# Sorted k of the late pairs copied into block order, so that the score matmuls read a block's columns side by side

## The chip, the cores and the metric

The kernel runs on one core of one Trainium2 chip. The metric is the time of one execution on the device, in microseconds (us). Most executions of this kernel agree within a few tenths of a per cent, but single ones are about 2 us longer with a mean granted TensorE clock of 0.99 in place of 1.00 (the kernel before, in one set of rounds: 226.22 us at 0.990 beside 223.60 to 224.78 at 0.997 and more; one more, 227.03 us at 0.990, was called slow and is left out of the ratios). Ratios in this document are the mean time of one kernel's fast runs over the mean of the other's fast runs of the same rounds, so they are not quite the ratios of the medians quoted beside them.

## The reference, cut to what matters

```python
# q, k, v: (4 batches, 8 heads, 768 positions, 64); sort_net: 8x8 per head; 8 blocks of 96 positions
for _ in range(5):                       # Sinkhorn normalisation of sort_net -> P
    ...
k_sorted = einsum('bhij,bhjcd->bhicd', P, k_b)   # mix the 8 blocks of k (and of v) by P
v_sorted = einsum('bhij,bhjcd->bhicd', P, v_b)
scores = scale * (q_block @ k_sorted_block^T)    # within each block only, 96 x 96
attn = softmax(scores)
x = (attn @ v_sorted_block)  -> (3072 tokens, 512)
out = square(relu(x @ w_in)) @ w_out             # 512 -> 2048 -> 512
```

The feed-forward part is most of the work. The attention of batch n+1 is woven into the feed-forward matmuls of batch n.

## The kernel before

A small planner inside the kernel decides the order of all instructions before anything runs. Each piece of work is given an engine, an estimated cost and the pieces it depends on. Pieces for TensorE also carry a due time, counted in chunks of feed-forward work. A transfer is a pseudo engine with a cost and a slack. In the traces VectorE, ScalarE and TensorE work their queues in order: what the planner puts first has to finish first, whatever really happens.

Two heads make a pair. For the ten late pairs (two of batch 1, four each of batches 2 and 3), k is sorted in natural order, transposed by a DMA from SyncE's queue, and lands in `kx` with the 8 blocks interleaved: column `8 x + i` belongs to block `i`. The score matmuls therefore read every eighth column:

```python
rkx, rkn, rqi = Ring(3), Ring(4), Ring(4)          # buffers: transposed k, natural k, paired q
...
def s_turn(b, hp):
    ...
    sp = plan.add("SP", 1.25, k_turn, [op, loaded(b)] + oldx)      # issue of the DMA transpose
    k_op = plan.add("WAY", 1.6, lambda e: None, [sp])              # its way, as planned
...
nc.tensor.matmul(out=scp[:, h, BLK * n:BLK * (n + 1)],
    lhsT=(u.ksT[64*h:64*(h+1), HS*hf + BLK*n:HS*hf + BLK*n + 128] if not u.tiled else
          kx_r[u.kx][64*h:64*(h+1), NQ*hf + n::NB]),               # step of 8 columns
    rhs=..., start=True, stop=True)
...
# sorted v of a batch: written to DRAM and read back in another layout, from SyncE's queue
slow = 6.0 if b == 1 else 2.0
there = plan.add("WAY", slow, ..., [wr]);  back = plan.add("WAY", slow, ..., [rd])
```

Early pairs have k in `kvT`, where a block's columns lie side by side. That gives a control inside the same trace.

The softmax here doesn't subtract the row's maximum and nothing guards it: scores larger than these inputs give would overflow.

Of the kernel before, what the change touches and what calls it, by code (L numbers as in the profile page):

```python
# [9 lines left out]
BF16 = mybir.dt.bfloat16  # L10
# [8 lines left out]


DUES = {
    (0, "K"): (-15.0, -1.0, 10, 10),
    (0, "S"): (-1.0, 11.0, 11.0, 15.0),
    (0, "T"): (-1.5, 10.0, 13.5, 19.5),
    (0, "A"): (14.0, 14.5, 18.0, 21.5),
    (0, "X"): (16.0, 23.0, 24.5, 25.0),
    (0, "W"): (1.5,),
    (1, "V"): (4.0, 20.5),
    (1, "Q"): (31.0,),
    (1, "N"): (None, 33.0),  # L30
    (1, "Z"): (None, None, 43.0, 44.0),
    (1, "S"): (33.5, 41.0, 43.0, 48.0),
    (1, "A"): (39.5, 41.5, 45.5, 52.0),
    (1, "X"): (48.0, 49.5, 49.5, 55.0),
    (2, "L"): (52.0,),
    (2, "N"): (64.0, 69.5),
    (2, "V"): (74.5, 91.5),
    (2, "Z"): (84.0, 86.0, 95.5, 96.5),
    (2, "S"): (88.5, 93.0, 97.5, 100.5),
    (2, "A"): (95.0, 99.5, 102.0, 104.0),  # L40
    (2, "X"): (96.5, 105.5, 107.5, 109.5),
    (3, "L"): (110.5,),
    (3, "N"): (120.0, 126.0),
    (3, "V"): (123.0, 141.5),
    (3, "Z"): (130.5, 138.0, 153.0, 155.5),
    (3, "S"): (143.5, 153.0, 157.5, 159.5),
    (3, "A"): (149.5, 155.0, 160.5, 162.5),
    (3, "X"): (158.5, 160.0, 161.5, 166.5),
}



FIRST = ("K0 V0 K1 v1 S0 t0 S1 k2 t1 A0 V2 S2 K3 t2 A1 V3 X0 A2 S3 t3 x1 A3 X2 x3")


class Op:
# [35 lines left out]
class Plan:  # L92
# [1 line left out]



    TAIL = {"PE": 0.0, "ACT": 0.09, "DVE": 0.06, "POOL": 0.0, "DMA": 0.0, "SP": 0.0, "WAY": 0.6}
    HOP = 0.06
    SWITCH = 0.1
    SLACK = {"DMA": 2.5, "WAY": 1.0}  # L100

    def __init__(self):
        self.att, self.ffn, self.rest = [], [], []
# [62 lines left out]
def kernel(  # L166
# [10 lines left out]
    nc = tc.nc  # L177

    B, H, S, D = q.shape
    NB = sort_net.shape[-1]  # L180
    BLK = S // NB
    NH = B * H
    NA = S // 128
    C0 = 128 // NB
    HP = H // 2
    NQ = NB // 2
    HS = S // 2
# [7 lines left out]
    const = ctx.enter_context(tc.tile_pool(name="const", bufs=1))  # L195
# [15 lines left out]
    plan = Plan()  # L211
    rvn, rvb = Ring(2), Ring(3)
    r1, r2, rf, rh1, rh2, rob = Ring(1), Ring(2), Ring(3), Ring(3), Ring(2), Ring(3)
    rqT, rao, rks, ret = Ring(6), Ring(3), Ring(3), Ring(4)
    rkx, rkn, rqi = Ring(3), Ring(4), Ring(4)
    AD = ("ACT", "DVE")

    def cost_f(n):
# [8 lines left out]
    def copy(eng, out, in_):  # L227
        if eng == "ACT":
            nc.scalar.copy(out=out, in_=in_)  # L229
        else:  # L230
            nc.vector.tensor_copy(out=out, in_=in_)  # L231
# [40 lines left out]
    v_way = nc.dram_tensor("v_way", (B, 2, NA, 128, HP * 66), BF16, kind="Internal").ap()  # L272

    kn_r = [const.tile([128, NA, 2, D], BF16, name=f"kn{n}") for n in range(4)]
    qi_r = [const.tile([128, NA, 2, D], BF16, name=f"qi{n}") for n in range(4)]
    kx_r = []
    for n in range(3):
        kx = const.tile([128, 128 * NB], BF16, name=f"kx{n}")
        nc.vector.memset(kx[:, 128 * NA:], 0.0)
        kx_r.append(kx)  # L280
    for n in range(4):
        et = const.tile([96, 2, HS + 32], BF16, name=f"et{n}")
        nc.vector.memset(et[:, :, HS:HS + 32], 0.0)
# [331 lines left out]
    def s_sc(u, due=0):  # L615

        u.exps = {}
        u.et = {}
        for hf in u.halves:
            st = {}  # L620

            slot, old = r2.take()

            def mm(e, hf=hf, st=st, slot=slot):
                qT = tiles["qT", u.b, u.hp]
                if not u.tiled:
                    qT = qT.rearrange("p a x -> p (a x)").rearrange("p (i q) -> p i q", q=BLK)
                st["p"] = scp = p2[slot]
                for n in range(NQ):
                    for h in range(2):  # L630
                        nc.tensor.matmul(  # L631
                            out=scp[:, h, BLK * n:BLK * (n + 1)],
                            lhsT=(u.ksT[64 * h:64 * (h + 1), HS * hf + BLK * n:HS * hf + BLK * n + 128]
                                  if not u.tiled else
                                  kx_r[u.kx][64 * h:64 * (h + 1), NQ * hf + n::NB]),
                            rhs=(qT[64 * h:64 * (h + 1), NQ * hf + n, :] if not u.tiled else
                                 qT[64 * h:64 * (h + 1), :, C0 * (NQ * hf + n):
                                    C0 * (NQ * hf + n + 1)]),
                            start=True, stop=True)

            s2 = slot
            u.et[hf], olde = ret.take()
            pe = plan.add("PE", 0.17 if not u.tiled else 0.26, mm, [u.k_op, u.q_op] + old, due,
                          mode="row")
            r2.use(s2, pe)
            rqT.use(qTs[u.b, u.hp], pe)
            if not u.tiled:
                rks.use(u.n, pe)
            else:
                rkx.use(u.kx, pe)  # L650
            u.exps[hf] = []
            if u.b == 0:
                def ex(e, st=st, et=et_r[u.et[hf]]):
                    nc.scalar.activation(out=et[:, :, 0:HS], in_=st["p"][0:96, :, 0:HS],  # L654
                                         func=AF.Exp, scale=scale)

                op = plan.add("ACT", cost_f(2 * HS)[0], ex, [pe] + olde)
                r2.use(s2, op)
                u.exps[hf].append(op)
                continue  # L660
            for h in range(2):
                def ex(e, h=h, st=st, et=et_r[u.et[hf]]):
                    nc.scalar.activation(  # L663
                        out=et[:, h, 0:HS].rearrange("p (n c a) -> p n c a", c=C0, a=NA),
                        in_=st["p"][0:96, h, 0:HS].rearrange("p (n a c) -> p n c a", c=C0, a=NA),
                        func=AF.Exp, scale=scale)
                op = plan.add("ACT", cost_f(HS)[0], ex, [pe] + olde)
                r2.use(s2, op)
                u.exps[hf].append(op)
# [28 lines left out]
    def s_nat(b, g, t, due):  # L698

        if t == 2:  # L700
            m, oldm = rvn.take()
        evs = []
        for hp in (2 * g, 2 * g + 1):
            slot, old = r2.take()
            if t == 1:
                m, oldm = rkn.take()
# [13 lines left out]
            def ev(e, hp=hp, slot=slot, m=m):  # L720
                dst = (vn_r[m][:, :, 2 * (hp % 2):2 * (hp % 2) + 2, 0:D] if t == 2
                       else kn_r[m])
                copy(e, dst, p2[slot][:, :, 0:NA * D].rearrange("p e (a d) -> p a e d", d=D))

            pe = plan.add("PE", 0.15, mm, [landed[b, t, HP * g, 0], built["t"]] + old, due,
                          mode="tile")
# [19 lines left out]
                in_=v_way[b, g].rearrange("a (c i) x -> (a c) (i x)", i=NB))  # L746

        wr = plan.add("SP", 0.33, write, evs + ([loaded(b)] if b > 1 else []))
        slow = 6.0 if b == 1 else 2.0
        there = plan.add("WAY", slow, lambda e: None, [wr])  # L750
        rd = plan.add("SP", 0.33, read, [there] + oldw)
        back = plan.add("WAY", slow, lambda e: None, [rd])
        rvn.use(m, *evs, there)
        rvb.use(w, back)
        v_blk[b, g] = w, back
# [4 lines left out]
    def s_turn(b, hp):  # L760

        m, op = k_nat[b, hp]
        kx, oldx = rkx.take()

        def k_turn(e):
            nc.sync.dma_start_transpose(
                out=kx_r[kx][:, 0:128 * NA].rearrange("p (a x) -> p a x", a=NA),
                in_=kn_r[m].rearrange("p a e d -> p (a e d)"))

        sp = plan.add("SP", 1.25, k_turn, [op, loaded(b)] + oldx)  # L770
        k_op = plan.add("WAY", 1.6, lambda e: None, [sp])
        rkn.use(m, k_op)
        rkx.use(kx, k_op)

        n, oldi = rqi.take()

        def q_pair(e):
            nc.vector.tensor_copy(
                out=qi_r[n].rearrange("p a e d -> p e a d"),
                in_=qkv[b][0][:, 2 * hp:2 * hp + 2, :].rearrange("p e (a d) -> p e a d", d=D))  # L780

        qp = plan.add("DVE", 0.5, q_pair, [landed[b, 0, HP * (2 * hp // HP), 0]] + oldi)
        readers[b].append(qp)
        rqi.use(n, qp)
        qTs[b, hp], oldq = rqT.take()

        def q_turn(e):
            tiles["qT", b, hp] = att.tile([128, NA, 128], BF16, tag="qT", name="qT", bufs=6)
            nc.sync.dma_start_transpose(
                out=tiles["qT", b, hp], in_=qi_r[n].rearrange("p a e d -> p (a e d)"))  # L790

        sp = plan.add("SP", 1.25, q_turn, [qp, loaded(b)] + oldq)
        q_op = plan.add("WAY", 1.6, lambda e: None, [sp])
        rqi.use(n, q_op)
        rqT.use(qTs[b, hp], q_op)
        return kx, k_op, q_op

    def s_av(u, due=0):
        nao, olda = rao.take()
# [44 lines left out]
    def s_xt(u, due=0, eng=AD):  # L844
        if u.b > 1 or u.b == 1 and u.hp < HP - 1:
            def turn(e):
                nc.sync.dma_start_transpose(
                    out=xT[:, u.hp, S * u.b:S * (u.b + 1)].rearrange("p (n q) -> p n q", q=BLK),
                    in_=u.ao.rearrange("p n e d -> p (n e d)"))

            sp = plan.add("SP", 1.25, turn, u.norms)
            op = plan.add("WAY", 1.6, lambda e: None, [sp])
            rao.use(u.nao, op)
            for hf in u.halves:
                x_done[u.b, u.hp, hf] = op
            return
# [251 lines left out]
```

## Time and profile before

| | before |
|---|---|
| time, median of the first three runs | 224.57 us (224.38 to 225.02) |
| span of the profiled execution | 222.0 us |
| TensorE busy | 213.3 us, 96% |
| VectorE, ScalarE busy | 46%, 54% |
| ten late pairs' score matmuls on TensorE | 7.03 us |
| longest data wait of TensorE after the start | 1.06 us, for sorted v of batch 3 |

The page and the timeline rows behind this table are shown and read in the prediction below. The one idea needed to read them is that TensorE works nearly all the time, so two things change the time: work that TensorE no longer has, and pauses in TensorE's queue.

To compare traces I also used a sum of pauses. For every row of TensorE's timeline after 21.5 us, I took the time to the start of the next row, less what its matmuls need undisturbed (0.1625 us per up-projection matmul and 0.216 per down-projection matmul, from 64 in 10.40 us and 48 in 10.36 us after 176 us in this trace, 0.44 or 0.63 per pair of score matmuls, and so on). For the kernel before the sum is 4.4 us. It is good to a few tenths.

### The profile page before, as it was taken

Reading aid. Unit: us, or ns where it says so; the run is one execution under the profiler, and the core shown is the slowest. Engines: PE = TensorE matmul, PEld = TensorE weight load, DVE = VectorE, ACT = ScalarE, POOL = GpSimd, SP = SyncE. Lnnn points to the kernel's source line nnn. Section 1 sums busy time; section 2 is a strip of 40 time slices with the busy share of each in tenths; the row PEclk is TensorE's granted clock in tenths of the full one; section 3 lists DMA queues with packets and bytes.
Section 4 is the critical chain, followed back from the end, with each engine's and each line's share of the span. In section 5 each row is a group of like instructions: output and inputs, shape, how many; then the busy total and the mean of one; then the engine's idle time right before and its main releaser. Section 6 shows DMA issues by size and latency. Waiting matters only on the chain.

```text
span 222.0 us, 5101 instructions
## 1 busy us (share of the span) xinstructions
PE 213.3 (96%) x2049; PEld 120.0 (54%) x2065; DVE 102.8 (46%) x291; ACT 120.8 (54%) x249; POOL 26.5 (12%) x49
## 2 busy tenths in 40 slices
PE   8998999999999999999999999999899999999993
PEld 2576666456665555445665465445555465455562
DVE  6768477444773347602676056404655155015300
ACT  4666888217976168517864178329573276147421
POOL 7973230000000600000000240000000000000000
PEclk9999999999999999999999999999999999999999
DMA  5999999998533499189943599648982510120012
GB/s 68 201 202 207 209 206 214 209 259 229 156 82 80 90 227 223 25 218 223 206 111 83 120 176 218 128 139 177 238 175 68 118 49 3 47 94 0 3 63 78
DMA packets 46583, 31.22 MB, mean 141 GB/s; under 512 B 26016, under 2 KB 41632, under 8 KB 46560
## 3 DMA queue, kind: packets, MB, share of 16 engines
q0 software_dynamic: 12736, 13.63, 37.2%
q1 hardware_dynamic: 33824, 17.27, 30.8%
q8 instruction: 16, 0.26, 0.5%
q14 instruction: 7, 0.06, 0.1%
HBM read 29.70 MB, written 8.72 MB: 173 GB/s over the span
## 4 chain that ended last, share of the span: by engine, by line
PE 75%; DMA 17%; POOL 4%; ACT 1%; issue 1%; DVE 1%; SPq 0%; ACTq 0%
PE op L921 33%; PE hp L893 31%; DMA vb<-in_v_dram 9%; DMA w_in_bf<-in_moe_w_in_dram 5%; PE p L631 3%; PE p L814 3%; DMA vblk<-v_way 2%; PE op L955 2%; PE p L714 2%; POOL vb L300 1%; POOL kb L300 1%; DMA p_sb<-in_sort_net_dram 1%; ACT h L901 1%; DVE h L904 1%; PE qtp L511 0%
## 5 line engine op out<-in xcount | busy, mean ns | idle before, releaser
L893 PE MATMUL hp<-xT,w_in_bf 128*128 128x384 bf16 x512 | 88.9, 326 | 0.0
L921 PE MATMUL op<-w_out_bf,h 128*128 128x512 bf16 x352 | 83.3, 379 | 0.9 <-issue 0.2
L904 DVE TENSOR_TENSOR h<-h 128x384 bf16<-128x384 bf16 x128 | 44.5, 356 | 62.7 <-ACT h L901 62.3
L901 ACT ACTIVATE h<-hp 128x384 bf16<-128x384 f32 x128 | 61.6, 495 | 19.1 <-PE hp L893 15.6
L893 PEld LDWEIGHTS <-w_in_bf 128*128 128x128 bf16 x512 | 48.1, 98 | 32.1 <-issue 1.0
L921 PEld LDWEIGHTS <-h 128*128 128x128 bf16 x368 | 34.0, 98 | 37.6 <-issue 0.9
L229 ACT COPY ob<-op 128x512 f32<-128x512 f32 (+1 forms) x24 | 13.6, 567 | 62.4 <-PE op L921 59.8
L825 DVE TENSOR_TENSOR ao<-p,rec 96x512 bf16<-96x512 f32 x32 | 22.0, 687 | 1.2
L663 ACT ACTIVATE et<-p 96x384 bf16<-96x384 f32 x48 | 19.5, 489 | 3.1 <-PE p L631 3.1
L814 PEld LDWEIGHTS <-et 96*128 96x128 bf16 x256 | 11.3, 97 | 5.5 <-issue 1.7
L824 DVE RECIPROCAL rec<-p 96x8 f32<-96x8 f32 x32 | 6.4, 199 | 16.4 <-PE p L814 16.2
L1047 POOL COPY held<-xT 1x3 bf16<-1x3 bf16 (+1 forms) x2 | 0.4, 183 | 89.2 <-DMA xT<-ao 89.2
L397 PE MATMUL p<-ones 128*128 128x512 bf16 (+1 forms) x36 | 10.0, 399 | 1.1 <-DVE ones L250 1.1
L814 PE MATMUL p<-vblk,et 96*128 96x65 bf16 x192 | 8.9, 193 | 1.1 <-DMA vblk<-v_way 1.1
L231 DVE CAST vn<-p 128x768 bf16<-128x768 f32 x6 | 5.7, 958 | 8.5 <-PE p L714 8.5
L631 PEld LDWEIGHTS <-kx 64*128 64x128 bf16 x160 | 6.1, 156 | 3.9 <-issue 3.7
L631 PE MATMUL p<-qT,kx 64*128 64x96 bf16 x160 | 7.4, 228 | 0.0
L231 DVE CAST kn<-p 128x768 bf16<-128x768 f32 x5 | 4.8, 957 | 4.8 <-PE p L714 4.8
L300 POOL DMA_DIRECT2D kb<-in_k_dram x10 | 6.4, 643 | 3.5 <-DMA w_in_bf<-in_moe_w_in_dram 2.0
L300 POOL DMA_DIRECT2D qb<-in_q_dram x8 | 6.1, 770 | 4.9 <-DMA w_out_bf<-in_moe_w_out_dram 2.1
L300 POOL DMA_DIRECT2D vb<-in_v_dram x10 | 6.3, 628 | 3.3 <-DMA w_in_bf<-in_moe_w_in_dram 2.0
L654 ACT ACTIVATE et<-p 96x768 bf16<-96x768 f32 x8 | 6.2, 804 | 0.1
(80 smaller groups left out, 112.9 us busy)
## 6 DMA issues: line engine op xcount, KB each, us to landing
out_dram<-ob SPq DMA_DIRECT2D x23, 256.0 KB, 2.2
qb<-in_q_dram POOLq DMA_DIRECT2D x8, 384.0 KB, 11.0
v_way<-vn SPq DMA_DIRECT2D x6, 396.0 KB, 4.2
vblk<-v_way SPq DMA_DIRECT2D x6, 396.0 KB, 4.1
vb<-in_v_dram POOLq DMA_DIRECT2D x6, 384.0 KB, 11.4
kb<-in_k_dram POOLq DMA_DIRECT2D x6, 384.0 KB, 10.0
w_in_bf<-in_moe_w_in_dram POOLq DMA_DIRECT2D x4, 512.0 KB, 11.8
w_out_bf<-in_moe_w_out_dram POOLq DMA_DIRECT2D x4, 512.0 KB, 18.9
```

The source lines that it names most:

```text
L229: nc.scalar.copy(out=out, in_=in_)
L231: nc.vector.tensor_copy(out=out, in_=in_)
L300: nc.gpsimd.dma_start(out=dst, in_=src)
L397: nc.tensor.matmul(out=out, lhsT=ones, rhs=rhs, start=True, stop=True)
L631: nc.tensor.matmul(out=scp[:, h, BLK * n:BLK * (n + 1)], lhsT=(u.ksT[64 * h:64 * (h + 1), HS * hf + BLK * n:HS * hf + BLK * n + 128] if no ...
L663: nc.scalar.activation(out=et[:, h, 0:HS].rearrange("p (n c a) -> p n c a", c=C0, a=NA), in_=st["p"][0:96, h, 0:HS].rearrange("p (n a c) - ...
L814: nc.tensor.matmul(out=oup[:, h, 66 * n:66 * n + D + 1], lhsT=et_r[u.et[hf]][:, h, BLK * n:BLK * n + 128], rhs=(u.vs[:, NQ * hf + n, h, 0: ...
L825: nc.vector.tensor_tensor(out=u.ao[:, n0:n0 + NQ, :, :].rearrange("p n e d -> p e n d"), in0=ov[:, :, :, 0:D], in1=rec[:, :, :, None].to_b ...
L893: nc.tensor.matmul(out=t["hp", nt][:, 0:HS], lhsT=w_in_bf[:, kc, 128 * nt:128 * (nt + 1)], rhs=xT[:, kc, t0:t0 + HS], start=(kc == 0), sto ...
L901: nc.scalar.activation(out=t["h1", nt], in_=t["hp", nt][:, 0:HS], func=AF.Relu)
L904: nc.vector.tensor_tensor(out=t["h2"][:, nt, :], in0=t["h1", nt], in1=t["h1", nt], op=ALU.mult)
L921: nc.tensor.matmul(out=t["op", mt], lhsT=t["h2"][:, nt, 128 * mt:128 * (mt + 1)], rhs=w_out_bf[:, nt, :], start=(nt == 0), stop=(nt == NT ...
```

## The change

The intent: let each engine do what it is good at. TensorE gets weights that lie side by side; the reordering goes to VectorE or ScalarE, which have time, as a copy that writes in order and reads with a step.

```diff
-    rkx, rkn, rqi = Ring(3), Ring(4), Ring(4)
+    rkx, rkn, rqi, rkc = Ring(2), Ring(4), Ring(3), Ring(3)
...
-                                  kx_r[u.kx][64 * h:64 * (h + 1), NQ * hf + n::NB]),
+                                  kc_r[u.kx][64 * h:64 * (h + 1),
+                                             HS * hf + BLK * n:HS * hf + BLK * n + 128]),
...
-        k_op = plan.add("WAY", 1.6, lambda e: None, [sp])
+        turned = plan.add("WAY", 2.2, lambda e: None, [sp])
+        kc, oldc = rkc.take()
+        def k_sort(e):
+            copy(e, kc_r[kc][:, 0:S].rearrange("p (i x) -> p i x", i=NB),
+                 kx_r[kx].rearrange("p (x i) -> p i x", i=NB))
+        k_op = plan.add(AD, (1.2, 1.2), k_sort, [turned] + oldc)    # ScalarE or VectorE
...
-        slow = 6.0 if b == 1 else 2.0          # sorted v through DRAM, "WAY" with slack 1.0
+        slow = 6.0 if b == 1 else 4.0          # "DRAM" with slack 0.5
...                                             # all other transposes: WAY 1.6 -> 2.2
-FIRST = ("K0 V0 K1 v1 S0 t0 S1 k2 t1 A0 V2 S2 K3 t2 A1 V3 X0 A2 S3 t3 x1 A3 X2 x3")
+FIRST = ("K0 V0 K1 V1 t0 S0 k2 S1 v2 t1 A0 S2 T2 k3 V3 A1 X0 A2 S3 t3 x1 A3 X2 x3")
...
 DUES: nearly all due times moved, for example
-    (3, "V"): (123.0, 141.5),
+    (3, "V"): (121.0, 136.0),
```

Three things thus come at once: the copy with packed weights, other planned transfer times (with the planner's tails, which set how soon the next transfer may start), and another order. The smaller rings come from memory: a variant with the old rings and the new `kc` buffers did not build, because the builder had 30.56 KB per partition left for one pool (`ffn`) that asked for 32.25.

More of the change, by code (lines that the diff above doesn't have):

```diff
@@ L21 @@
 DUES = {
-    (0, "K"): (-15.0, -1.0, 10, 10),
-    (0, "S"): (-1.0, 11.0, 11.0, 15.0),
-    (0, "T"): (-1.5, 10.0, 13.5, 19.5),
-    (0, "A"): (14.0, 14.5, 18.0, 21.5),
-    (0, "X"): (16.0, 23.0, 24.5, 25.0),
-    (0, "W"): (1.5,),
-    (1, "V"): (4.0, 20.5),
-    (1, "Q"): (31.0,),
-    (1, "N"): (None, 33.0),
-    (1, "Z"): (None, None, 43.0, 44.0),
-    (1, "S"): (33.5, 41.0, 43.0, 48.0),
-    (1, "A"): (39.5, 41.5, 45.5, 52.0),
-    (1, "X"): (48.0, 49.5, 49.5, 55.0),
-    (2, "L"): (52.0,),
-    (2, "N"): (64.0, 69.5),
-    (2, "V"): (74.5, 91.5),
-    (2, "Z"): (84.0, 86.0, 95.5, 96.5),
-    (2, "S"): (88.5, 93.0, 97.5, 100.5),
-    (2, "A"): (95.0, 99.5, 102.0, 104.0),
-    (2, "X"): (96.5, 105.5, 107.5, 109.5),
-    (3, "L"): (110.5,),
-    (3, "N"): (120.0, 126.0),
-    (3, "V"): (123.0, 141.5),
-    (3, "Z"): (130.5, 138.0, 153.0, 155.5),
-    (3, "S"): (143.5, 153.0, 157.5, 159.5),
-    (3, "A"): (149.5, 155.0, 160.5, 162.5),
-    (3, "X"): (158.5, 160.0, 161.5, 166.5),
+    (0, "K"): (-10.0, -8.0, 6, 6.0),
+    (0, "S"): (-1.0, 11.5, 12.0, 16.0),
+    (0, "T"): (1.5, 10.0, 16.5, 19.0),
+    (0, "A"): (14.5, 16.5, 16.5, 24.0),
+    (0, "X"): (14.5, 16.5, 22.5, 24.0),
+    (0, "W"): (0.0,),
+    (1, "V"): (2.5, 19.5),
+    (1, "Q"): (26.5,),
+    (1, "N"): (None, 36.5),
+    (1, "Z"): (None, None, 44.5, 38.0),
+    (1, "S"): (33.0, 39.0, 46.5, 51.0),
+    (1, "A"): (42.5, 42.5, 47.0, 52.5),
+    (1, "X"): (43.5, 49.5, 53.0, 54.5),
+    (2, "L"): (58.0,),
+    (2, "N"): (67.5, 75.0),
+    (2, "V"): (68.5, 91.5),
+    (2, "Z"): (81.0, 84.0, 95.0, 87.5),
+    (2, "S"): (86.5, 93.0, 99.0, 99.0),
+    (2, "A"): (96.0, 98.0, 101.0, 104.5),
+    (2, "X"): (97.5, 99.5, 107.0, 108.0),
+    (3, "L"): (111.0,),
+    (3, "N"): (132.5, 128.5),
+    (3, "V"): (121.0, 136.0),
+    (3, "Z"): (135.0, 145.0, 150.0, 152.0),
+    (3, "S"): (144.5, 153.0, 158.5, 160.0),
+    (3, "A"): (147.0, 155.0, 159.5, 162.0),
+    (3, "X"): (156.5, 163.5, 163.5, 164.5),
 }
-FIRST = ("K0 V0 K1 v1 S0 t0 S1 k2 t1 A0 V2 S2 K3 t2 A1 V3 X0 A2 S3 t3 x1 A3 X2 x3")
+FIRST = ("K0 V0 K1 V1 t0 S0 k2 S1 v2 t1 A0 S2 T2 k3 V3 A1 X0 A2 S3 t3 x1 A3 X2 x3")
 class Op:
@@ L92 @@
 class Plan:
-    TAIL = {"PE": 0.0, "ACT": 0.09, "DVE": 0.06, "POOL": 0.0, "DMA": 0.0, "SP": 0.0, "WAY": 0.6}
+    TAIL = {"PE": 0.0, "ACT": 0.09, "DVE": 0.06, "POOL": 0.0, "DMA": 0.0, "SP": 0.0, "WAY": 1.0, "DRAM": 3.0}
     HOP = 0.06
     SWITCH = 0.1
-    SLACK = {"DMA": 2.5, "WAY": 1.0}
+    SLACK = {"DMA": 2.5, "WAY": 1.0, "DRAM": 0.5}
     def __init__(self):
@@ L274 @@
     kn_r = [const.tile([128, NA, 2, D], BF16, name=f"kn{n}") for n in range(4)]
-    qi_r = [const.tile([128, NA, 2, D], BF16, name=f"qi{n}") for n in range(4)]
-    kx_r = []
+    qi_r = [const.tile([128, NA, 2, D], BF16, name=f"qi{n}") for n in range(3)]
+    kx_r = [const.tile([128, 128 * NA], BF16, name=f"kx{n}") for n in range(2)]
+    kc_r = []
     for n in range(3):
-        kx = const.tile([128, 128 * NB], BF16, name=f"kx{n}")
-        nc.vector.memset(kx[:, 128 * NA:], 0.0)
-        kx_r.append(kx)
+        kc = const.tile([128, S + 32], BF16, name=f"kc{n}")
+        nc.vector.memset(kc[:, S:S + 32], 0.0)
+        kc_r.append(kc)
     for n in range(4):
@@ L642, in s_sc @@
             u.et[hf], olde = ret.take()
-            pe = plan.add("PE", 0.17 if not u.tiled else 0.26, mm, [u.k_op, u.q_op] + old, due,
+            pe = plan.add("PE", 0.17 if not u.tiled else 0.18, mm, [u.k_op, u.q_op] + old, due,
                           mode="row")
@@ L649, in s_sc @@
             else:
-                rkx.use(u.kx, pe)
+                rkc.use(u.kx, pe)
             u.exps[hf] = []
@@ L748, in s_nat @@
         wr = plan.add("SP", 0.33, write, evs + ([loaded(b)] if b > 1 else []))
-        slow = 6.0 if b == 1 else 2.0
-        there = plan.add("WAY", slow, lambda e: None, [wr])
+        slow = 6.0 if b == 1 else 4.0
+        there = plan.add("DRAM", slow, lambda e: None, [wr])
         rd = plan.add("SP", 0.33, read, [there] + oldw)
-        back = plan.add("WAY", slow, lambda e: None, [rd])
+        back = plan.add("DRAM", slow, lambda e: None, [rd])
         rvn.use(m, *evs, there)
@@ L770, in s_turn @@
         sp = plan.add("SP", 1.25, k_turn, [op, loaded(b)] + oldx)
-        k_op = plan.add("WAY", 1.6, lambda e: None, [sp])
-        rkn.use(m, k_op)
-        rkx.use(kx, k_op)
+        turned = plan.add("WAY", 2.2, lambda e: None, [sp])
+        rkn.use(m, turned)
+        kc, oldc = rkc.take()
[3 more added lines that the diff above has]
+        k_op = plan.add(AD, (1.2, 1.2), k_sort, [turned] + oldc)
+        rkx.use(kx, turned, k_op)
+        rkc.use(kc, k_op)
         n, oldi = rqi.take()
@@ L792, in s_turn @@
         sp = plan.add("SP", 1.25, q_turn, [qp, loaded(b)] + oldq)
-        q_op = plan.add("WAY", 1.6, lambda e: None, [sp])
+        q_op = plan.add("WAY", 2.2, lambda e: None, [sp])
         rqi.use(n, q_op)
         rqT.use(qTs[b, hp], q_op)
-        return kx, k_op, q_op
+        return kc, k_op, q_op
     def s_av(u, due=0):
@@ L851, in s_xt @@
             sp = plan.add("SP", 1.25, turn, u.norms)
-            op = plan.add("WAY", 1.6, lambda e: None, [sp])
+            op = plan.add("WAY", 2.2, lambda e: None, [sp])
             rao.use(u.nao, op)
```

## The prediction

> **What bounds the kernel now.** I read the totals and the slices first, then the groups kept apart by shape, the timeline of TensorE, and last the chain that ended last. The totals and slices of the page:
>
> ```profile
> PE 213.3 (96%) x2049; PEld 120.0 (54%) x2065; DVE 102.8 (46%) x291; ACT 120.8 (54%) x249; POOL 26.5 (12%) x49
> ...
> PE   8998999999999999999999999999899999999993
> PEld 2576666456665555445665465445555465455562
> DVE  6768477444773347602676056404655155015300
> ACT  4666888217976168517864178329573276147421
> ```
>
> TensorE works in every slice at 90% and more, except at the start and the end. VectorE and ScalarE are half idle. So the time is TensorE's work plus the few gaps in its queue; moving time onto or off VectorE and ScalarE costs nothing unless it makes TensorE wait. The groups by shape give the disputed matmuls and the nearest relatives of the new copy:
>
> ```profile
> L631 PE MATMUL p<-qT,kx 64*128 64x96 bf16 x160 | 7.4, 228 | 0.0
> ...
> L631 PEld LDWEIGHTS <-kx 64*128 64x128 bf16 x160 | 6.1, 156 | 3.9 <-issue 3.7
> ...
> L631 PE MATMUL p<-qT,kvT 64*128 64x96 bf16 x96 | 3.6, 204 | 0.2 <-DVE ao L825 0.2
> ...
> L778 DVE COPY qi<-qb 128x768 bf16<-128x768 bf16 x10 | 3.1, 353 | 0.0
> ...
> L631 PEld LDWEIGHTS <-kvT 64*128 64x128 bf16 x96 | 2.4, 94 | 1.7 <-issue 1.4
> ```
>
> Both kinds of score matmul have one shape. Those of the early pairs take their weights from kvT, where the columns of a block lie side by side; those of the ten late pairs (2 of batch 1, 4 each of batches 2 and 3) take them from kx with a step of 8 elements, 16 bytes. A weight load takes 156 ns there against 94. Since matmuls overlap, what counts is not the duration but when TensorE goes on to its next job. From TensorE's timeline (columns: start, length, then the group; the start of the next row is what to read):
>
> ```profile
> 56.93 0.51 PE L631 MATMUL p<-qT,kvT 64*128 64x96 bf16 x16
> 57.37 2.12 PE L893 MATMUL hp<-xT,w_in_bf 128*128 128x384 bf16 x12
> ...
> 103.20 0.69 PE L631 MATMUL p<-qT,kx 64*128 64x96 bf16 x16
> 103.83 2.12 PE L893 MATMUL hp<-xT,w_in_bf 128*128 128x384 bf16 x12
> ...
> 153.39 2.77 PE L893 MATMUL hp<-xT,w_in_bf 128*128 128x384 bf16 x16
> 157.23 0.66 PE L814 MATMUL p<-vblk,et 96*128 96x65 bf16 x16 [1.06 <-DMA vblk<-v_way]
> ```
>
> A pair of 16 score matmuls holds TensorE for 57.37 - 56.93 = 0.44 us from kvT and for 103.83 - 103.20 = 0.63 us from kx. The last row is the longest wait for data after the start: 1.06 us for sorted v of batch 3. In the chain that ended last it stands as:
>
> ```profile
> 152.19 0.44 SPq L766
> 152.63 0.05 issue
> 152.68 0.02 SPq L744
> 152.69 0.03 issue
> 152.72 4.46 DMA vblk<-v_way
> 157.19 0.04 issue
> 157.23 0.66 PE p L814 x16
> ```
>
> Behind a transpose in SyncE's queue the read of v was issued at 152.7 and took 4.46 us.
>
> [...]
> [...]the trace has 94 to 98 ns for unit steps.[...]
> [...]
> [...]the page of before has 798 ns for ScalarE copies of 768 elements out of PSUM.
>
> **The change, part by part.**
> Removed: the strided weight loads. In the timeline the ten kx pairs hold TensorE for 0.87, 0.90, 0.63, 0.65, 0.83, 0.64, 0.63, 0.62, 0.63 and 0.63 us, 7.03 in all. The seven undisturbed ones average 0.633; the other three have a pause between their halves. If a packed pair takes the 0.44 of kvT, the ten save 10 x (0.633 - 0.44) = 1.93 us, all on TensorE's path. One difference stays: the late pairs' moving operand still comes in runs of 16 columns, and their matmuls take 228 against 204 ns, which may keep a little. I count 1.8 us.
> Added: ten copies of 128x768. On ScalarE I estimate 0.83 us from the 798 ns above;[...] the 16-byte reads may add some. Ten at 0.9 are 9 us over two engines that together are idle for 222 - 103 + 222 - 121 = 220 us. None lies on TensorE's queue. What counts is latency: sorted k is ready about 1 us later, after a transpose that takes 2.5 to 4.3 us to land (median 3.6). The late pairs' k is transposed several pairs ahead except for the first pair of each batch: in batch 3 the first transpose goes out at 147.3 and its scores start at 152.76. With 4.3 to land and 0.9 to copy it is ready at 152.5, just in time.
> Moved: the order of TensorE's and SyncE's work. The planned transfer times grow (2.2 for 1.6 us per transpose, 4 for 2 us per pass of v through DRAM), so reads of sorted v are planned later than they were, and batch 3's second v sort is due 5.5 chunks earlier (136 for 141.5; a chunk is 0.65 us of up projection or 0.87 of down). The measured 4.46 us for the read shows that the old plan was too hopeful, the new one is not. The 1.06 us should mostly go: I count 0.8. The pauses in three pairs, 0.87 + 0.90 + 0.83 - 3 x 0.633 = 0.70, are accidents of order; I count half, 0.3.
> The start, up to the first up projection at 22.48 us, gets another order and other engines for five evictions. Adding up from the groups' durations (0.48 to 0.80 on ScalarE, 0.36 to 0.89 on VectorE), both engines carry about 7.0 us before and 7.1 to 7.2 after in the ten us from the first sort on. I count zero, plus or minus 0.7. The memsets of the zero columns get smaller, outside any path.
> New waits: +0.4 for sorted copies that come late or a relu held up behind a copy.
> Sum: -1.8 - 0.8 - 0.3 + 0.4 = -2.5 us on 224.57, so 222.1; I say 222.0.
>
> **The rivals.**
> First, the moving operand sets the pace, not the weights: 16 matmuls of 96 columns in 0.63 us are 39 ns each[...]. Against it: kvT does the same columns at 27 ns each[...]. If it held, the change would save only the waits: 223.5 to 224.5.
> Second, the longer way of k becomes the bound: TensorE's queue is in order, so a late copy stalls everything behind it. Three batches of late pairs could lose 1 us each at their first pair, and TensorE saves nothing on balance: 224 to 226. For it: the 152.5 against 152.76 above. Against it: the first scores of batch 3 are due a chunk later and the plan allows more for the transposes.
> Third, copies in ScalarE's queue hold up relu. In an up projection a relu of 0.50 comes every 0.65 us, so a copy of 0.83 us is paid off only over five or six tiles; three PSUM buffers give about 1.3 us of slack, enough for one copy, not for one together with four exponentials (1.62 us). The slice with ScalarE at 9 lies at 150 to 155 us, just there. It would cost some 0.3 us a time, at most 2 in all: 223 to 224.
> Fourth, the new order also fills the remaining gaps. From 22.48 to the last matmul at 218.2 there are 195.7 us; the feed-forward matmuls at 162.5 ns (384 columns) and 216 ns (512) make 166.4 of it, the attention work I add up to some 24.6, so about 4.7 us are gaps. If most went besides the 1.9, the time would be 218 to 219.
>
> **Range and chances.** The sure part is 1.8 us of 224.57, 0.8%; the waits are worth from -2.5 to +2. That gives 219.9 to 224.2 for eight times in ten. Faster by over 2% means under 220.1, which needs the fourth rival: 0.11. Slower by over 2% means a lost 4.5 us with the saving on top: 0.03. Within 2%: 0.86.
>
> **What would show it.** Weight loads of the late pairs at 94 to 98 ns for 156, and 0.44 to 0.47 us from a pair's first matmul to TensorE's next job, for 0.63. Ten new copies of 0.8 to 1.0 us, TensorE never listed as waiting for them beyond 0.3 us. No wait of about 1 us for vblk. The first up projection within 0.7 us of 22.48. TensorE's busy time lower by 1 to 2 us. I am wrong if the loads get short and the pairs stay at 0.63 (first rival), if scores wait for the copies (second), if matmuls of the up projection wait for relu (third), or if the start moves by more than a microsecond.

What no trace or run of this case shows is cut from the recorded prediction, and each cut is marked: statements on steps, weight loads and copies, the author's estimate for a copy on VectorE, a rate for 96 columns and a clause on weight loads in the first rival, which e1 tests. The 94 to 98 ns are loads of 128 columns (94 from kvT, 97 from et, 98 from w_in and h). The 0.83 and 0.9 us a copy are estimates. For a queue of TensorE in order (second rival) the trace has the 1.06 us before 157.23: the up-projection matmuls behind the weighted sum waited with it.

## The result, and the profile after

| | before | after |
|---|---|---|
| time, median of 4 | 224.59 us (224.38 to 225.02) | 228.01 us (227.84 to 228.70) |
| ratio of fast runs | | 1.0155 (95%: 1.013 to 1.0181) |
| span of the profiled execution | 222.0 us | 226.9 us |
| sum of pauses of TensorE after 21.5 us | 4.4 us | 10.4 us |

The changed kernel is 3.4 us slower by the medians, outside the predicted range; the ratio is clear of 1 but under 2%. The two traces differ by 4.9 us, because the profiled run after was the slowest of its four (228.70) and the one before was a quick one (223.75).

The page's totals and slices after:

```profile
PE 213.6 (94%) x2071; PEld 118.0 (52%) x2071; DVE 107.9 (48%) x297; ACT 127.8 (56%) x253; POOL 26.5 (12%) x49
...
PE   8897999899999999999969999999899999999993
```

TensorE's slices now have a 6 in the middle; before, that stretch was all nines. VectorE has 5 us more work and ScalarE 7 us more. The groups by shape (busy us in total, mean ns of one, then the idle time before them):

```profile
L230 ACT COPY kc<-kx 128x768 bf16<-128x768 bf16 x5 | 7.9, 1578 | 4.9 <-DMA kx<-kn 4.9
...
L634 PE MATMUL p<-qT,kc 64*128 64x96 bf16 x160 | 5.8, 204 | 0.2 <-ACT kc L230 0.2
...
L232 DVE COPY kc<-kx 128x768 bf16<-128x768 bf16 x5 | 4.2, 848 | 5.2 <-DMA kx<-kn 5.2
...
L634 PEld LDWEIGHTS <-kc 64*128 64x128 bf16 x160 | 3.9, 94 | 5.0 <-issue 3.2 <-ACT kc L230 0.7 <-DVE h L916 0.6
```

The weights do what was hoped: 94 ns a load for 156, and 204 ns a matmul for 228. But two other things stand here. A copy on ScalarE takes 1578 ns, about double the estimate. And VectorE stood idle 5.2 us, ScalarE 4.9 us, in front of their copies, waiting for the transposes. TensorE's timeline shows where that goes:

```profile
105.36 0.51 PE L634 MATMUL p<-qT,kc 64*128 64x96 bf16 x16
105.80 1.47 PE L905 MATMUL hp<-xT,w_in_bf 128*128 128x384 bf16 x8
...
112.12 0.81 PE L905 MATMUL hp<-xT,w_in_bf 128*128 128x384 bf16 x4
115.25 0.41 PE L826 MATMUL p<-vblk,et 96*128 96x65 bf16 x8 [2.32 <-DVE ao L837]
...
163.87 0.66 PE L826 MATMUL p<-vblk,et 96*128 96x65 bf16 x16 [1.07 <-DMA vblk<-v_way]
```

A late pair holds TensorE for 105.80 - 105.36 = 0.44 us, as predicted. At 113 us TensorE then waits 2.32 us for a normalisation (`ao`) on VectorE. Nothing in that normalisation has to do with k. The timeline of VectorE at that moment says why it was late:

```profile
108.88 1.32 DVE L916 TENSOR_TENSOR h<-h 128x384 bf16<-128x384 bf16 x4
113.53 0.84 DVE L232 COPY kc<-kx 128x768 bf16<-128x768 bf16 x1 [3.32 <-DMA kx<-kn]
114.28 0.20 DVE L836 RECIPROCAL rec<-p 96x8 f32<-96x8 f32 x1
114.52 0.69 DVE L837 TENSOR_TENSOR ao<-p,rec 96x512 bf16<-96x512 f32 x1
```

The copy had reached the head of VectorE's queue at 110.2 and its transpose landed only at 113.5. For 3.32 us VectorE did nothing, although normalisations whose matmuls were done at 111.4 stood right behind the copy. ScalarE stood the same way, idle for 2.54 us in front of its own copy at 115.10; the relu behind it came only at 117.23. The 1.07 us wait for sorted v of batch 3 is still there too. In batch 3, ScalarE's copies at 165.1 and 169.3 stand ahead of exponentials, and TensorE waits 0.43 and 0.35 us for those.

Why was the transpose late? SyncE's timeline after, and below it the same place before:

```profile
94.84 4.20 SPq L949 DMA_DIRECT2D out_dram<-ob  x2
99.14 0.39 SPq L742 DMA_DIRECT2D v_way<-vn  x1
99.58 1.70 SPq L770 DMA_TRANSPOSE kx<-kn  x1
...
108.21 1.24 SPq L770 DMA_TRANSPOSE kx<-kn  x1
```

```profile
94.41 0.33 SPq L937 DMA_DIRECT2D out_dram<-ob  x1
...
95.27 1.71 SPq L766 DMA_TRANSPOSE kx<-kn  x1
```

In the order of the changed plan, a second output store stands ahead of batch 2's first transpose, which goes out at 99.58. In the trace before it went out at 95.27, behind one store, although TensorE is only 1.5 us behind at that point (down projection of the third unit: 90.6 against 89.1). Each transpose then takes SyncE some 1.25 us to issue, and the third k transpose of the batch, sent at 108.21, took 5.3 us to land (before, none took over 4.3); why it took so long was not tested.

### The profile page after: what moved, and what is told of

The parts are those of the page before. It is cut to its first block, busy times and chain, and to the rows that moved or that the text cites. A ratio compares the mean times of both kernels' runs of the same rounds, so it can differ in the third digit from the quotient of the medians.

```text
span 226.9 us, 5129 instructions
## 1 busy us (share of the span) xinstructions
PE 213.6 (94%) x2071; PEld 118.0 (52%) x2071; DVE 107.9 (48%) x297; ACT 127.8 (56%) x253; POOL 26.5 (12%) x49
## 4 chain that ended last, share of the span: by engine, by line
PE 66%; DMA 19%; POOL 4%; DVE 3%; ACT 3%; issue 2%; ACTq 0%; DVEq 0%
PE op L933 32%; PE hp L905 27%; DMA vb<-in_v_dram 9%; DMA w_in_bf<-in_moe_w_in_dram 5%; DMA kx<-kn 2%; DMA vblk<-v_way 2%; DVE ao L837 2%; PE p L826 2%; PE p L718 2%; PE p L634 2%; PE op L967 2%; ACT et L667 1%; POOL vb L303 1%; POOL kb L303 1%; ACT h L913 1%
## 5 line engine op out<-in xcount | busy, mean ns | idle before, releaser
L933 PE MATMUL op<-w_out_bf,h 128*128 128x512 bf16 x368 | 86.3, 379 | 0.9 <-DMA w_out_bf<-in_moe_w_out_dram 0.6
L933 PEld LDWEIGHTS <-h 128*128 128x128 bf16 x368 | 33.5, 98 | 37.8 <-issue 2.0
L230 ACT COPY ob<-op 128x512 f32<-128x512 f32 (+1 forms) x23 | 13.0, 567 | 52.0 <-PE op L933 49.3
L826 PE MATMUL p<-vblk,et 96*128 96x65 bf16 x192 | 9.4, 193 | 4.2 <-DVE ao L837 2.3
L230 ACT COPY kc<-kx 128x768 bf16<-128x768 bf16 x5 | 7.9, 1578 | 4.9 <-DMA kx<-kn 4.9
L232 DVE COPY kc<-kx 128x768 bf16<-128x768 bf16 x5 | 4.2, 848 | 5.2 <-DMA kx<-kn 5.2
```

Of the source, the lines that this page charges most:

```text
L230: nc.scalar.copy(out=out, in_=in_)
L232: nc.vector.tensor_copy(out=out, in_=in_)
L826: nc.tensor.matmul(out=oup[:, h, 66 * n:66 * n + D + 1], lhsT=et_r[u.et[hf]][:, h, BLK * n:BLK * n + 128], rhs=(u.vs[:, NQ * hf + n, h, 0: ...
L933: nc.tensor.matmul(out=t["op", mt], lhsT=t["h2"][:, nt, 128 * mt:128 * (mt + 1)], rhs=w_out_bf[:, nt, :], start=(nt == 0), stop=(nt == NT ...
```

## The experiments

The theory after reading the traces: the packed weights save what was predicted, and the copies lose more, because a copy that waits for a late transpose at the head of an in-order queue holds up relu, squares, exponentials and normalisations behind it. Rivals: the new order and the new planned times cost by themselves; the copies cost by their length; the packed weights save nothing. Twelve kernels ran. Times are medians; "before" is the kernel before, run in the same rounds (for e9 to e12, seven of its eight runs are those of e1 to e4). The rounds ran on three chips: e6 to e8 on a second, e13 on a third, the others on the first; the kernel before took 224.2 to 224.6 us on each, so the changed kernel's 228.01 us, whose chip is not on record, is set beside all of them. All passed the comparison with the reference, even those that are wrong: q and k are drawn at a tenth of unit size, so the attention weights are nearly equal and this comparison does not see k well. That the other edits are right rests on reading them.

| run | time, us | before, us | ratio (95%) |
|---|---|---|---|
| packed weights, no copy (e1) | 223.07 | 224.63 | 0.9937 (0.9882 to 0.9992) |
| copies from a finished tile (e2) | 224.56 | 224.63 | 1.0007 (0.9945 to 1.0070) |
| short copies (e3) | 225.63 | 224.63 | 1.0054 (0.9992 to 1.0115) |
| new order, old way of k (e4) | 224.86 | 224.63 | 1.0020 (0.9968 to 1.0073) |
| copies on GpSimd, same order (e6) | 225.29 | 224.22 | 1.0031 (0.9946 to 1.0116) |
| copies, old order (e7) | 229.09 | 224.22 | 1.0187 (1.0119 to 1.0254) |
| copies on GpSimd, old order (e8) | 226.54 | 224.22 | 1.0061 (0.9981 to 1.0142) |
| copies planned on GpSimd (e9) | 229.85 | 224.47 | 1.0242 (1.0162 to 1.0323) |
| the same, transposes earlier (e10) | 226.30 | 224.47 | 1.0088 (1.0031 to 1.0146) |
| copies planned later (e11) | 232.18 | 224.47 | 1.0339 (1.0284 to 1.0395) |
| before, one due time changed (e12) | 223.09 | 224.47 | 0.9942 (0.9901 to 0.9983) |
| copies with unit step (e13) | 226.09 | 224.59 | 1.0053 (0.9985 to 1.0122) |

**e1: packed weights without a copy.**

```diff
 (kernel before)
-  kx_r[u.kx][64 * h:64 * (h + 1), NQ * hf + n::NB]
+  kx_r[u.kx][64 * h:64 * (h + 1), HS * hf + BLK * n:HS * hf + BLK * n + 128]
```

> The kernel before, in its own order, with one edit: the score matmuls of the late pairs read 128 columns of kx side by side instead of every eighth (the wrong columns, so the result is wrong on purpose); no copy, no new order. Theory (the strided weight load costs 0.19 us a pair): weight loads at 94 ns, ten pairs at 0.44 us, time 224.6 - 1.9 = 222.7 (222.3 to 223.1). Rival (the moving operand's short runs set the pace): loads get short, pairs stay near 0.63, time 224.2 to 224.8.

Measured: weight loads at 94 ns, matmuls at 204 ns, and 223.07 us, 1.56 below the kernel before (the interval of the ratio allows 0.2 to 2.7 us). The rival that the moving operand sets the pace falls: the operand is the same, and the pairs take 0.44 us wherever nothing else disturbs them. The saving is 0.4 short of the expected 1.9, within the expected range. In this trace the wait for sorted v of batch 3 is 1.68 us instead of 1.06: TensorE arrives earlier and waits for the same transfer, so about 0.6 of the 1.9 us is given back there.

**e2: copies that never wait.**

```diff
 (changed kernel, same order)
-  copy(e, kc..., kx_r[kx].rearrange("p (x i) -> p i x", i=NB))
+  copy(e, kc..., w_all[:, 0:6, :, :].rearrange("p h i c -> p (h i c)")
+                     .rearrange("p (x i) -> p i x", i=NB))      # finished long before
```

> The changed kernel in exactly its order, but the ten copies read a tile that was finished long before (wrong result on purpose), so no copy waits for a transpose at the head of VectorE's or ScalarE's queue; their number, size and stride stay. Theory (copies that wait for a late transpose block the in-order queue behind them): the 2.3 us wait at 113 us goes and most of what it delays, time 228.0 - 2.5 to - 3.5 = 224.5 to 225.5. Rival (the copies' own 0.85 and 1.58 us, or the new order, cost the time): 227 to 228.5.

Measured: 224.56 us, 3.45 below the changed kernel. The copies still take 1578 and 851 ns, their number and their place in the queues are the same, and the 2.3 us wait is gone. The theory holds for the bulk. This edit also frees the scores from waiting for k, but in the changed kernel TensorE's matmuls waited only 0.2 us in all for a copy, so that is a small part.

**e3: copies of 96 columns.**

```diff
 (changed kernel, same order)
-  copy(e, kc[.. i, x], kx[.. i, x])
+  copy(e, kc[.. i, 0:12], kx[.. i, 0:12])      # and kc cleared whole at the start
```

> The changed kernel in exactly its order, the copies still waiting for their transposes but moving 96 of 768 columns (wrong result on purpose). Theory (waiting, not copying, costs most): only the exponentials that queue behind ScalarE's 1.58 us copies in batch 3 get better, time 228.0 - 0.5 to - 1.3 = 226.7 to 227.5. Rival (the length of the copies is the cost): 224 to 225.5.

Measured: 225.63 us, 2.4 below the changed kernel: far more than the theory allowed, and just short of the rival's range. The copies take 360 and 242 ns. VectorE still waits 2.92 us for kx at 112 us, but TensorE's wait there is 1.32 instead of 2.32 us and the two waits for exponentials in batch 3 are gone. My reading is that length and waiting do not add up: the queue is blocked for the wait plus the length, and removing either lets the same work through. So "waiting, not copying" was too simple.

**e4: the new order with the old way of k.**

```diff
 (changed kernel)
-  k_op = the copy into kc;  lhsT = kc, side by side;  kx ring of 2
+  k_op = the transpose;     lhsT = kx, step of 8;     kx ring of 3
```

> The changed kernel's due times, order of the first batch, planned transfer times and rings, but with the old way of k: strided reads of kx, no copy (right result). If the new order by itself costs (start later by 0.5 to 1.4, reads of sorted v later): 225.5 to 226.5. If the copies alone are to blame: 224.0 to 224.8.

Measured: 224.86 us against 224.63. The new order and planned times by themselves are not slower within the interval (the median is 0.06 above the range expected for this case). They start batch 2's transposes late here too (98.5 us), but no copy stands in another engine's queue to wait for them. So from this kernel to the changed one the copies cost 228.01 - 224.86 = 3.15 us net, and some 3.15 + 1.56 = 4.7 us gross of what e1 showed the packing to save. This is no surer than e1's saving, which is good to about 1.2 us, and the changed kernel has one kx buffer fewer than this one.

**e6: the same order, copies on GpSimd.**

```diff
 (changed kernel; planned as before, issued elsewhere)
-  copy(e, ...)
+  nc.gpsimd.tensor_copy(...)
```

> The changed kernel with the ten copies given to GpSimd, which is idle there; the order on TensorE, VectorE (less the copies), ScalarE and SyncE stays. Right result. Theory (a copy that waits at the head of an in-order queue blocks the work behind it, and the long ScalarE copies add to it): nothing waits behind a GpSimd queue that has no other work, so 228.0 - 3 to - 4.5 = 223.5 to 225.0, the rest being scores that wait for slower GpSimd copies. Rival (late transposes stall TensorE at the scores themselves): 226.5 or more, with score matmuls waiting for kc.

Measured: 225.29 us, 2.7 below the changed kernel, a little above the expected range. TensorE's timeline:

```profile
113.15 0.81 PE L905 MATMUL hp<-xT,w_in_bf 128*128 128x384 bf16 x4
115.78 0.34 PE L634 MATMUL p<-qT,kc 64*128 64x96 bf16 x8 [1.82 <-POOL kc L780]
```

The normalisation no longer waits, but now the scores themselves meet an unfinished copy. A GpSimd copy takes 1.6 us, for 0.85 on VectorE and 1.58 on ScalarE. So both hold: blocking was the larger cost, and the longer way of k is the next one.

**e7: copies on VectorE and ScalarE, with the due times and planned transfer times of the kernel before.**

```diff
 (changed kernel)
-  DUES, FIRST, WAY 2.2, DRAM 4.0 of the changed kernel;  copy planned at (1.2, 1.2)
+  those of the kernel before (1.6 and 2.0);              copy planned at (1.6, 0.87)
```

> The copies on VectorE and ScalarE (planned at their measured 0.87 and 1.6 us), but due times, order of the first batch and planned transfer times of the kernel before; rings as in the changed kernel, as memory allows no more. Right result. If the new order is what makes the transposes of batches 2 and 3 late, copies wait less and the time is 223 to 225; if planning too short transfer times makes the copies block their queues even more, 227 to 230.

Measured: 229.09 us, in the range expected for planned times that are too short. It is 1.1 above the changed kernel, but the intervals of the two ratios overlap, so it is not shown to be worse. It is no better although batch 2's first transpose goes out early here, at 95.56 (its first scores start at 103.48, in the changed kernel at 105.36). From the list of who waited for whom (us in total, times, longest):

```profile
DVE kc L231 <- DMA kx<-kn: 9.7, 4, 5.6
...
ACT kc L229 <- DMA kx<-kn: 3.2, 1, 3.2
...
PE hp L904 <- ACT h L912: 3.0, 1, 3.0
```

One copy stood 3.2 us at the head of ScalarE's queue, relu stood behind it, and TensorE waited 3.0 us for that relu. It is the same fault on the other engine. Whether the longer planned times of the changed kernel help a little is not shown.

**e8: as e7, with the copies on GpSimd, planned there at 2.0 us.**

```diff
 (e7)
-  k_op = plan.add(AD, (1.6, 0.87), k_sort, ...);  copy(e, ...)
+  k_op = plan.add("POOL", 2.0, k_sort, ...);      nc.gpsimd.tensor_copy(...)
```

> As the last, but the copies on GpSimd, planned at 2.0 us. Right result. Theory: strided loads gone (-1.5 as measured without copies), no blocked queue, transposes early: 223.0 to 224.3, below both kernels. Rival (the longer way of k stalls the scores): 224.6 to 226.

Measured: 226.54 us (224.28 to 227.21; two of the four runs at a clock of 0.99, which widens it). The blocked queues are gone, some 2.5 us better than e7, but the kernel before is not beaten. In its trace, one of the two at 0.99, the wait for sorted v is 2.36 us. In the page's slice in which it ends (157.7 to 163.3 us) the clock is 0.6, and the 32 matmuls after the wait hold TensorE for 4.72 us, where 3.09 is undisturbed. This was a miss; the rival (224.6 to 226) is nearer.

**e9: the changed kernel's due times, copies planned on GpSimd at 1.65 us.**

```diff
-  k_op = plan.add(AD, (1.2, 1.2), k_sort, ...);   copy(e, ...)
+  k_op = plan.add("POOL", 1.65, k_sort, ...);     nc.gpsimd.tensor_copy(...)
```

> The changed kernel with its own due times and planned transfer times, the ten copies on GpSimd and planned there at their measured 1.65 us, so that the order of the scores knows of them. Right result. Theory: no queue blocked, scores no longer meet an unfinished copy (1.8 us in the run with GpSimd in the changed kernel's order): 223.3 to 224.8. Rival (the longer way of k is the bound whatever the plan): 225 to 226.5.

Measured: 229.85 us; both expectations missed. GpSimd and VectorE at 112 us, each from its own timeline:

```profile
112.60 3.18 POOL L780 COPY kc<-kx 128x768 bf16<-128x768 bf16 x2 [5.52 <-DMA kx<-kn]
```

```profile
112.83 1.54 DVE L916 TENSOR_TENSOR h<-h 128x384 bf16<-128x384 bf16 x1
114.29 0.19 DVE L836 RECIPROCAL rec<-p 96x8 f32<-96x8 f32 x1
```

A square that takes 0.36 us took 1.54, about as long as one of the two GpSimd copies beside it (3.18 us). In all four kernels with copies on GpSimd the longest square is 1.72 to 1.77 us, in the changed kernel 0.36; why a square takes longer there is not shown. The long square held relu (ScalarE waited 2.44 us for it), and relu held TensorE for 0.98 us. Then three score groups stood in a row: TensorE waited 0.69 and 0.41 us for exponentials and 1.40 us for a relu that stood behind eight of them (3.15 us) in ScalarE's queue, which is the order of the plan and not the square. Meanwhile the clock went. The columns of this answer are the stretch, its length, the busy time of TensorE, weight loads, VectorE, ScalarE and GpSimd, then the granted clock, the DMA share and GB/s:

```profile
116.00:118.00 2.00, 0.90 (x28) 0.61 (x24) 0.84 (x4) 1.78 (x5) 0.00 (x0) 0.96 0.55 175
118.00:120.00 2.00, 0.60 (x9) 0.39 (x7) 0.22 (x1) 2.00 (x7) 0.00 (x0) 0.50 0.59 126
120.00:122.00 2.00, 2.00 (x14) 0.98 (x13) 0.85 (x3) 0.50 (x2) 0.00 (x0) 0.50 0.00 0
122.00:124.00 2.00, 2.00 (x14) 0.93 (x12) 1.69 (x4) 0.00 (x0) 0.00 (x0) 0.50 0.04 8
```

TensorE was busy for 1.5 of 4 us, and its clock was 0.50 from about 117.8 to 124.7 us, although it was busy again from 119.8 on. An estimate from these rows: 4.6 us of busy time from 118 to 124 at half the clock lost 2.3 us. The mean clock was 0.983 to 0.993 in all four runs of e9, so its 229.85 us are not the cost of the copies alone.

**e10: as e9, with less slack after loads, so that the transposes stand earlier in SyncE's order.**

```diff
-  SLACK = {"DMA": 2.5, ...
+  SLACK = {"DMA": 0.5, ...
```

> As the last, but the plan allows 0.5 us instead of 2.5 us after a load, so that in SyncE's order the transposes of batches 2 and 3 stand ahead of an output store that holds them up now. Right result. Theory (late start of the transposes, not their length, makes k late): first transpose of batch 2 some 3 us earlier, time 222.8 to 224.3, at or below the kernel before. Rival (loads land later than planned and the queue stalls): 225 or more.

Measured: 226.30 us, 3.5 below e9; the theory's 222.8 to 224.3 is missed, and the number is the rival's. The first transpose of batch 2 goes out at 95.26 instead of some 99 us and batch 2 runs without a long pause: between 100 and 125 us the sum of pauses falls from 7.7 us in e9 (some of it the slow clock) to 1.7. Batch 3 then loses 2.57 us at the wait for sorted v, whose read stands in the same queue. So earlier transposes removed the long pauses of batch 2 in this plan, but not enough to reach the kernel before.

**e11: copies on VectorE and ScalarE, planned 2.5 us later.**

```diff
+  sure = plan.add("WAY", 2.5, lambda e: None, [turned])
-  k_op = plan.add(AD, (1.2, 1.2), k_sort, [turned] + oldc)
+  k_op = plan.add(AD, (1.6, 0.87), k_sort, [sure] + oldc)
```

> The changed kernel with the copies on VectorE and ScalarE, planned at their measured 0.87 and 1.6 us and 2.5 us later than now, so that they stand further back in the queues and find their data there. Right result. Theory (the wait at the head of the queue is the cost): no engine waits over 1 us for kx, time 224.3 to 226.0. Rival (copies on these engines cost it by their length): 227 or more.

Measured: 232.18 us, the slowest of all. The theory's range is missed; the number is in the rival's, but not for the rival's reason. No wait of VectorE or ScalarE for kx is left among its waits, as the theory said. But TensorE pays elsewhere:

```profile
PE hp L906 <- DMA xT<-ao: 5.3, 3, 2.0
```

With k later, the attention of a batch ends later, and the next feed-forward unit waits for its input, 5.3 us in three waits at the ends of batches 2 and 3. After the first two of them the clock, too, is lower, 0.7 in the page's slice from 132.5 to 138.3 us, and 61 up-projection matmuls hold TensorE for 11.59 us, where 9.91 is undisturbed. So a copy placed early blocks a queue, and a copy placed late delays the batch. In this kernel there is not enough time between the loads and the next unit for the longer way.

**e12: the kernel before with one due time changed.**

```diff
-    (3, "A"): (149.5, 155.0, 160.5, 162.5),
+    (3, "A"): (152.5, 155.0, 160.5, 162.5),
```

> The kernel before with one due time changed: the first weighted sum of batch 3 three chunks later (152.5 for 149.5), so that TensorE has feed-forward work while sorted v comes back; this asks how much the 1.06 us wait, which the change did not remove, is worth. Right result. If only that wait goes: 223.3 to 224.1 against 224.2 to 224.6. If the wait turns up again a little later: no change.

Measured: 223.09 us against 224.47, ratio 0.9942, the interval below one, 0.2 us below the expected range. It beats both kernels, by less than 2%. TensorE has 28 up-projection matmuls in the place where it had 16 and a wait:

```profile
153.45 4.72 PE L893 MATMUL hp<-xT,w_in_bf 128*128 128x384 bf16 x28
158.12 0.65 PE L814 MATMUL p<-vblk,et 96*128 96x65 bf16 x16
```

**e13: the copies read with a step of one.**

```diff
 (changed kernel, same order)
-  kx_r[kx].rearrange("p (x i) -> p i x", i=NB)
+  kx_r[kx].rearrange("p (i x) -> p i x", i=NB)     # wrong columns
```

> The changed kernel in exactly its order, the ten copies of 768 columns still waiting for their transposes, but reading kx column by column instead of with a step of 8 (the wrong columns, wrong result on purpose). If the 16-byte step is what makes ScalarE's copy 1.58 us: 0.80 to 0.85 us there; on VectorE 0.25 to 0.40 us for 0.85. Time: between the run with short copies (225.6) and the changed kernel (228.0), 225.5 to 226.7, as the waits stay. If ScalarE stays at 1.58, the step is not the cause and the time stays above 227 too.

Measured: 829 ns a copy on ScalarE for 1578, 355 ns on VectorE for 848, and 226.09 us. The time is in the expected range. So the 16-byte step doubles ScalarE's copy, and copies of half the length or less save 228.01 - 226.09 = 1.9 us in this order, for the reason given under e3.

One version could not be tried: sorting k so that four columns of a block lie side by side in `kx` and no copy is needed. It did not build: the builder refused such weights, as they had two free dimensions and it takes one.

## Why the prediction was wrong

- **"-1.8" for the packed weights** was right. The loads take 94 ns and the pairs 0.44 us. In the time, e1 showed 1.56, with 0.6 more waiting for v. The sign "TensorE's busy time lower by 1 to 2 us" did not come (213.6 for 213.3), but the two pages hold different numbers of matmul records (2071 and 2049), so it decides nothing.
- **"None lies on TensorE's queue. What counts is latency"** is the step that failed. The prediction asked when sorted k would be ready for the scores, and the term "New waits: +0.4" of its sum is the one that was wrong: about 4.7 us were lost in its place (e4 to the changed kernel, with the packing's saving added back). It took the wait of a copy for a wait of k alone. A waiting copy takes its whole engine with it: e2, which removes the waiting and keeps the copies, is 3.45 us faster. The 3.32 us in front of the copy, with finished work behind it, show it directly.
- **The second rival** (the longer way of k as bound, 224 to 226) named the right source, a transpose that lands too late, but the wrong pair (it was the third of batch 2, not the first of a batch) and the wrong victim: it foresaw late scores. Scores late by more than 0.2 us appear only once the queue is free (e6, 1.82 us).
- **The third rival** (copies hold up relu in ScalarE's queue) was put at 2 us at most, counting only a copy's length. With the waiting added it cost 3.0 us at one place in e7.
- **"On ScalarE I estimate 0.83 us"** was mis-sized: 1.58 us. The 798 ns it came from were reads out of PSUM without the step. For VectorE, whose estimate is cut, 0.85 us was measured.
- **"Should mostly go: I count 0.8"** for the v wait was wrong: 1.07 us remains. The longer planned time moved the sum later, but the read of v went out later as well (158.97 against 152.72 us) in a queue that was later altogether.
- **"I count zero, plus or minus 0.7"** for the start was missed by a little: the first up projection starts at 23.40 instead of 22.48, 0.92 later. More sorting is done before it, so both kernels reach the first down projection at 37.6, and e4 shows no net loss from the order.
- **Slips that change nothing.** The saving of 1.8 with waits from -2.5 to +2 gives 220.3 to 224.8, not "219.9 to 224.2". TensorE was not at 90% in every slice: the one from 155 to 161 us, where it waits for sorted v, is an 8. ScalarE has a second 9, at 55 to 61 us.

What stays open is how the 1.3 us that remain between e2 and an undisturbed packed kernel (224.86 - 1.56 = 223.3) divide between the copies' length and chance in the transfers. Nor is it shown that no plan could make the copy pay; the six plans tried here did not. The nearest one, the changed kernel on VectorE and ScalarE with the earlier transposes of e10, was not run. Nor is it shown what lowers the clock: a wait of 3.04 us in e7 and one of 2.57 us in e10 left it at 1.00, in the slice in which one of 2.36 us in e8 ends it is 0.6, and in e9 it dropped at about 117.8 us with no wait longer than 0.98 us in the 8 us before it, when TensorE had been busy for 2.9 of the 5 us from 113 to 118.

## What to carry to other kernels

Work moved to an idle engine was not free here, because it waited there (3.45 us, e2) and stood long in front of urgent work (2.4 us, e3): ask for each new instruction what it waits for, when that really arrives, and what stands behind it in that engine's queue. If a late transfer feeds it, try an engine whose queue has nothing urgent behind it (2.7 us better in e6), and look there at how long the other engines' instructions now take (squares of up to 1.77 us for 0.36). And before buying a new saving, look at the pauses that are already there: one due time gave about as much here as the whole packing.
